# Second MLP of an attention and two-MLP kernel: seven products in one run, then 36 output products in one run

## The chip, the cores and the metric

The kernel runs on one core of one Trainium2 chip. The metric is device time in microseconds (us); before the change the median of three runs is 923.41 (922.23 to 925.97). Nothing is computed on the host.

## What is computed

Kernelized attention for 4 batches of 8 heads, 576 tokens and 64 features; its output, laid out as 2304 tokens of 512 features, goes through two MLPs. The second one is what the change touches:

```python
def _moe_ref(x, w1, w2, w3, w_out):
    a = x @ w1                         # 512 -> 1024
    b = x @ w2
    h = a * b @ w3
    return h @ w_out                   # 1024 -> 512

def _moe2_ref(x, w_in, w_out):
    h = x @ w_in                       # 512 -> 2048
    r = np.maximum(h, 0.0)
    g = r * r
    return g @ w_out                   # 2048 -> 512
```

The second MLP's weights arrive as 64-bit words and are decoded to float32 on the chip.

## The kernel before

**Three stages.** Attention (to about 210 us in the trace), the first MLP (to about 528) and the second MLP (to the end). Each float32 operand is split in a high and a low half, and each product of two tiles is three matmuls (high by high, low by high, high by low; `passes`). Each matmul is preceded by its own weight load, which overlaps the matmul before.

**First MLP.** 40 steps of 36 matmuls (of 512 columns where the batch has 512 tokens): 12 for `pa`, 12 for `pb`, and 12 that fold the gated product g of the step before into four accumulators `yp` (line 984, `fold_part`; here called the fold products). VectorE makes g from `pb` and the copy of `pa`, ScalarE its high half, VectorE its low half (line 1145). In the last two runs of steps the accumulators are added to a partial sum read back from HBM (`yp<-y_part`, line 972). The result goes to HBM as `y_hbm`, in three slabs of 768 tokens.

**Decoding beside it.** The weights of the second MLP are decoded in 32 items, 28, 29, 23 and 26 among the last; the table `many` (line 929) says how many items begin in each step. An item costs VectorE five operations of 128x512 and one or more for its low half, and the results are stored in HBM (`pair_hbm<-w_w`, `<-v_w`, line 809).

**Second MLP.** A slab has 16 blocks of 128 hidden features, taken in eight pairs p; over the three slabs there are 24 pairs q. For a pair the hidden layer is computed with seven products instead of eight (a Strassen-Winograd scheme): the seven *forms* of the slab's activations (b11, t2, b21, t3, t1, b22, t4: sums and differences of quarters, split in halves, tiles yf_b and yf_t) are multiplied by forms of the weights (a11, s2, a12, s3, s1, s4, a22). Each product is six matmuls of 384 columns (line 1221) into one of three banks x (`ph_x`), y (`ph_y`) and w (`ph_w`), where x and y are each added to later: x takes a11 and a12, y takes s2, s3 and a22, w takes s1 and s4. Between them the other engines form the sums: ScalarE copies x to m after a11; VectorE makes u = y + m after s2, m5 = w + m + y, and later w + u and y + m. Each of the four results is squared after a maximum with zero on VectorE (line 1236), its high half r is made on ScalarE (line 1232) and its low half on VectorE (line 1233). Then the 36 output products of 512 columns of that pair (line 1247, `op<-pair,r`: r times the weights `wo`) accumulate into six banks op_0 to op_5 over the eight pairs of a slab; they are issued during the next pair.

**What sets the order.** No scheduler: within the manual sections the instructions stand on each engine in the order in which the program issues them, and a wait holds everything behind it on that engine. `filling` is a list of output products of the pair before; `fill(4)`, `fill(3)`, `fill(2)` and `fill(1)` issue a quarter, a third of the rest, and so on, between the products. The weights of the pairs are loaded by `pump` (line 1056) on SP, in the order of `coming_pairs`, when room for two tiles is free; the first calls stand in `first_forms` (line 933), which also says after which step of the first MLP (30 to 39) each form of the first slab is made. `pair` of tiles 0 and 1 are the seven products' weights (two tiles each, 0_0, 0_1, 1_0, 1_1), 2 and 3 are `wo`.

At the end of a slab (its pairs 6 and 7, and the first pair of the next) the next slab's sums and forms are made between the products (`adding`, `remake`). The last six output tiles are copied out of their banks on ScalarE and VectorE in turn and stored by halves of 64 rows, on SP's and on ScalarE's queue (`put_out`).

## Time and profile before

| | us |
|---|---|
| median of three runs | 923.41 |
| profiled execution | 924.3 |
| its span, first to last instruction | 922.5 |
| TensorE busy | 900.5 |
| VectorE busy | 670.8 |
| ScalarE busy | 379.0 |
| mean granted TensorE clock | 0.995 of 2.4 GHz |

Busy time of TensorE counts a matmul until its modelled end, which overlaps the next one: a busy TensorE need not be at its peak, and the distance between the starts of groups tells more. The chain of waits follows the work back from the last instruction, at each step to what released it. In the timeline a row holds a run of like instructions: its start, its length, and in brackets the idle time before it with what ended that. PEld is the weight load, SPq and ACTq are the issues of transfers on SP and ScalarE.

### The profile page before, as it was taken

Reading aid. Unit: us, or ns where it says so; the run is one execution under the profiler, and the core shown is the slowest. Engines: PE = TensorE matmul, PEld = TensorE weight load, DVE = VectorE, ACT = ScalarE, POOL = GpSimd, SP = SyncE. Lnnn points to the kernel's source line nnn. Section 1 sums busy time; section 2 is a strip of 40 time slices with the busy share of each in tenths; the row PEclk is TensorE's granted clock in tenths of the full one; section 3 lists DMA queues with packets and bytes.
Section 4 is the critical chain, followed back from the end, with each engine's and each line's share of the span. In section 5 each row is a group of like instructions: output and inputs, shape, how many; then the busy total and the mean of one; then the engine's idle time right before and its main releaser. Section 6 shows DMA issues by size and latency. Waiting matters only on the chain.

```text
span 922.5 us, 15634 instructions
## 1 busy us (share of the span) xinstructions
PE 900.5 (98%) x6012; PEld 764.1 (83%) x6012; DVE 670.8 (73%) x1214; ACT 379.0 (41%) x709; POOL 159.5 (17%) x240
## 2 busy tenths in 40 slices
PE   8999999999999999999999989999999999999997
PEld 6777777778888888988888778989898998889896
DVE  6988888879978797789999656476754447554443
ACT  4777777653433434444455322222421213312121
POOL 2666666453222530000000000000000000000000
PEclk9999999999999999999999989999999999999999
DMA  6455465456452346848895967777675675676442
GB/s 190 123 151 157 139 162 153 120 149 160 105 170 83 122 117 213 287 158 248 293 353 205 356 233 269 240 276 249 224 251 206 209 269 179 215 264 226 168 160 68
DMA packets 120089, 182.60 MB, mean 198 GB/s; under 512 B 60304, under 2 KB 79312, under 8 KB 120016
## 3 DMA queue, kind: packets, MB, share of 16 engines
q1 hardware_dynamic: 118912, 180.66, 60.6%
q8 instruction: 47, 0.77, 0.3%
q10 hardware_dynamic: 1104, 0.95, 0.3%
q14 instruction: 26, 0.21, 0.1%
HBM read 140.54 MB, written 40.89 MB: 197 GB/s over the span
## 4 chain that ended last, share of the span: by engine, by line
PE 82%; DVE 8%; DMA 4%; ACT 4%; issue 1%; SPq 0%; ACTq 0%; DVEq 0%
PE op L1247 20%; PE pb L221 10%; PE yp L984 9%; PE pa L221 9%; PE ph_y L1221 7%; PE ph_x L1221 5%; PE ph_w L1221 5%; PE pf L910 5%; PE po L495 2%; PE pk L282 2%; PE pkv L468 2%; PE pq L407 2%; PE pd L515 1%; ACT qp L457 1%; DMA mrow<-mh 1%
## 5 line engine op out<-in xcount | busy, mean ns | idle before, releaser
L1247 PE MATMUL op<-pair,r 128*128 128x512 f32 x864 | 214.8, 393 | 0.0
L1247 PEld LDWEIGHTS op<-pair,r 128*128 128x128 f32 x864 | 161.9, 188 | 29.5
L984 PE MATMUL yp<-g,w3o 128*128 128x512 f32 (+1 forms) x480 | 105.6, 368 | 0.0
L984 PEld LDWEIGHTS yp<-g,w3o 128*128 128x128 f32 x480 | 84.1, 189 | 14.9 <-DVE w3o L187 0.2
L1232 ACT ACTIVATE r<-m 128x384 fp32r<-128x384 f32 x48 | 25.2, 525 | 168.7 <-DVE m L1236 168.7
L221 PE MATMUL pa<-c,w_w12a 128*128 128x512 f32 (+1 forms) x432 | 94.1, 366 | 0.2 <-ACT c L186 0.2
L221 PE MATMUL pb<-c,w_w12b 128*128 128x512 f32 (+1 forms) x432 | 93.6, 366 | 0.0
L1221 PE MATMUL ph_y<-yf_t,pair 128*128 128x384 f32 x432 | 89.2, 341 | 1.8 <-DVE u L1291 1.8
L221 PEld LDWEIGHTS pa<-c,w_w12a 128*128 128x128 f32 x432 | 75.1, 189 | 14.0 <-ACT c L186 0.6
L221 PEld LDWEIGHTS pb<-c,w_w12b 128*128 128x128 f32 x432 | 75.2, 189 | 13.1
L1221 PEld LDWEIGHTS ph_y<-yf_t,pair 128*128 128x128 f32 x432 | 77.8, 191 | 4.8 <-DVE u L1291 2.1
L1221 PE MATMUL ph_x<-yf_b,pair 128*128 128x384 f32 x288 | 59.3, 340 | 3.5 <-ACT m L1287 1.8
L1221 PEld LDWEIGHTS ph_x<-yf_b,pair 128*128 128x128 f32 x288 | 51.7, 191 | 6.9 <-ACT m L1287 2.8
L1143 ACT ACTIVATE g<-g 128x512 fp32r<-128x512 f32 (+1 forms) x39 | 23.0, 589 | 81.8 <-DVE g L1141 81.8
L540 POOL TENSOR_SCALAR rc<-dc 32x9 f32<-32x9 f32 x128 | 44.9, 350 | 55.7 <-DVE dc L530 48.6
L399 ACT ACTIVATE kp<-kp 128x512 f32<-128x512 f32 (+1 forms) x80 | 46.9, 588 | 16.4 <-DVE kp L392 14.4
L1233 DVE TENSOR_TENSOR r<-m,r 128x384 fp32r<-128x384 f32 x48 | 26.8, 559 | 28.4 <-ACT r L1232 28.4
L910 PE MATMUL pf<-w_wo,w3T 128*128 128x512 f32 x192 | 45.0, 390 | 0.0
L1316 DVE TENSOR_TENSOR m<-ph_w,m 128x384 f32<-128x384 f32 x24 | 13.3, 556 | 40.0 <-PE ph_w L1221 40.0
L910 PEld LDWEIGHTS pf<-w_wo,w3T 128*128 128x128 f32 x192 | 36.0, 188 | 7.5
L123 DVE SCALAR_TENSOR_TENSOR dt_w<-raw_w,dt_w 128x512 int32<-128x512 int32 x48 | 39.1, 814 | 1.6
L1141 DVE TENSOR_TENSOR g<-pb,a 128x512 f32<-128x512 f32 (+1 forms) x39 | 24.7, 634 | 19.8 <-PE pb L221 19.5
(169 smaller groups left out, 1528.0 us busy)
## 6 DMA issues: line engine op xcount, KB each, us to landing
pair<-pair_hbm SPq DMA_DIRECT2D x144, 512.0 KB, 6.4
pair_hbm<-w_w SPq DMA_DIRECT2D x32, 512.0 KB, 7.6
raw_w<-in_moe_w_in_dram SPq DMA_DIRECT2D x16, 512.0 KB, 4.0
raw_w<-in_moe_w_out_dram SPq DMA_DIRECT2D x16, 512.0 KB, 5.4
pair_hbm<-v_w SPq DMA_DIRECT2D x16, 512.0 KB
raw_w<-in_moe_w_dram SPq DMA_DIRECT2D x56, 128.0 KB, 3.2
x<-x_hbm SPq DMA_DIRECT2D x12, 512.0 KB
yi<-y_hbm SPq DMA_DIRECT2D x12, 384.0 KB, 8.0
```

The source lines that it names most:

```text
L123: nc.vector.scalar_tensor_tensor(out=t, in0=hi, scalar=-(1 << 31), in1=t, op0=ALU.bitwise_and, op1=ALU.bitwise_or)
L221: nc.tensor.matmul(ps[:, 0:n], a, c, start=kk + i == 0, stop=kk == KD - 1 and i == 2)
L399: nc.scalar.activation(z["kp", j][:, :, s, :], z["kp", j][:, :, 1, :], AF.Exp, scale=1.0 - 2.0 * s)
L540: nc.gpsimd.tensor_scalar(out=z["rc2"][i * 32:(i + 1) * 32, s, :], in0=z["dc"][at * 32:(at + 1) * 32, :], scalar1=1e-6, scalar2=None, op0= ...
L910: nc.tensor.matmul(pf, a, c, start=n == 0, stop=n == len(todo) - 1)
L984: nc.tensor.matmul(blk.yp[i][:, 0:blk.n], a, d, start=c == blk.c0 and s == 0, stop=c == blk.c1 - 1 and s == 2)
L1141: nc.vector.tensor_tensor(out=g32[:, 0:n], in0=pb[:, 0:n], in1=a_sb[:, 0:n], op=ALU.mult)
L1143: nc.scalar.activation(g[:, 0, 0:n], g32[:, 0:n], AF.Copy)
L1221: nc.tensor.matmul(ps_, a, c, start=start and n == 0, stop=n == 5, skip_group_check=not start)
L1232: nc.scalar.activation(r[:, 0], h, AF.Copy)
L1233: nc.vector.tensor_tensor(out=r[:, 1], in0=h, in1=r[:, 0].bitcast(F32), op=ALU.subtract)
L1247: nc.tensor.matmul(z.ops[i], a, d, start=z.p + j + s == 0, stop=z.p == NP2 - 1 and j == 1 and s == 2)
```

## The change

The work is the same, product for product. What is changed is its order, in five places.

1. *Most pairs.* In the first pair, the last, and the pairs 1 to 6 of each slab (`whole`) the seven products come in one run (with a22 ahead of s4), then the output products of the pair before in one run, op_4 and op_5 first. All four squarings (t's among them, now a maximum with zero once more and a product in one operation) stand behind the seventh product on VectorE, then the next slab's sums where due, then the decoding of weights (`work`). Pairs 0 and 7 of a slab keep the old order, but for pair 0 of the first slab and pair 7 of the last.
2. *Put-off squarings.* After pair 0 two, and after pair 7 of a slab one of the four results are left in tiles of their own (`put_off`) and squared during the next pair, behind its u (`done_later`).
3. *The hand-over from the first MLP.* The last fold products come behind all seven products of pair 0; the adds of `yp` to the partial sum are spread between the sums of pair 1 (`carried`).
4. *First forms and loads.* `first_forms` and `many` change, and with them the order of decoded items, of the first slab's forms and of the loads on SP.
5. *The end.* The last output tile is copied by columns, half on VectorE and half on ScalarE, and stored from both queues; the two tiles before it go out on SP alone.

```diff
     many = [
-        2, 2, 2, 2, 2, 2, 2, 2, 2, 1, 2, 2, 1, 1, 1, 1, 0, 1, 2, 0, 0, 0, 1, 0, 2, 2, 1, 2,
+        2, 2, 2, 2, 2, 2, 2, 2, 2, 1, 2, 2, 1, 1, 1, 1, 0, 0, 2, 0, 1, 0, 1, 0, 2, 2, 1, 2,
...
     first_forms = {
-        30: ["load"],
+        31: ["load"],
         32: ["sums", "b22"],
...
-        38: ["b21", "give", "pump0"],
-        39: ["pump1"],
+        37: ["t1", "pump0"],
+        38: ["t4", "pump1"],
+        39: ["b21", "give"],
...
+        if last and i == 2:
+            half = C * D
+            nc.vector.tensor_copy(o[:, 0:half], op[:, 0:half])
+            nc.scalar.copy(o[:, half:], op[:, half:])
+            nc.sync.dma_start(dst[0][:, 0:half], o[:, 0:half])
+            nc.scalar.dma_start(dst[0][:, half:], o[:, half:])
+            return
...
-            (queue_of if last else nc.sync).dma_start(dst[0][half] if len(dst) == 1 else dst[h], o[half])
+            (queue_of if last and i > 2 else nc.sync).dma_start(dst[0][half] if len(dst) == 1 else dst[h], o[half])
...
+        def put_off(z, at):
+            later.append((z, at))
+            room_t[1] -= 1
+            name = f"h_{z.nm}_{at[0]}_{at[1]}"
+            z.h[at] = pools[1].tile([P, 512], I32, tag="dt", bufs=4, name=name).bitcast(F32)[:, 0:WIDE]
...
-                filling += [lambda z=before, i=i, j=j: out_part(z, i, j) for i in range(6) for j in range(2)]
+                filling += [lambda z=before, i=i, j=j: out_part(z, i, j) for i in (4, 5, 0, 1, 2, 3) for j in range(2)]
...
             nc.vector.tensor_tensor(out=u2, in0=y, in1=m1, op=ALU.add)
+            if later:
+                done_later()
             product(x, a12, "b21", False)
...
+            whole = q in (0, last) or p not in (0, NP2 - 1)
+            if whole:
+                nc.vector.tensor_tensor(out=m5, in0=y, in1=m1, op=ALU.add)
+            else:
...
+            if q == 1:
+                carried(range(1))
             x = bank_of(pre, "pre", f"ph_w_{z.nm}")[:, 0:WIDE]
             product(x, s1, "t1", True)
...
+            nc.vector.tensor_tensor(out=m5, in0=x, in1=m5, op=ALU.add)
+            if q == 1:
+                carried(range(1, 4))
+            while later:
+                done_later()
+            if whole:
+                product(y, a22, "t4", False)
+                squared(z, (0, 0))
+                if q == 0:
+                    put_off(z, (0, 1))
+                    put_off(z, (1, 0))
+                nc.vector.tensor_tensor(out=z.h[1, 0], in0=y, in1=m1, op=ALU.add)
+                product(x, s4, "b22", False)
+                nc.vector.tensor_tensor(out=z.h[0, 1], in0=x, in1=u2, op=ALU.add)
+                squared(z, (1, 1))
+                for at in ((0, 1), (1, 0)) if q else ():
+                    squared(z, at)
+                give(*[t_ for x_ in range(2) for t_ in fed[x_]])
+                fill(1)
+                if adding:
+                    wide_sums(raws)
+                work()
```

TensorE in a full pair, here pair 3, from its fourth product on; a row is a run of like matmuls, with tile numbers at the names' ends. Before:

```order
L1221 MATMUL ph_y_3_6723<-yf_t_0_6117,pair_0_1_6568 128x384 x3
L1221 MATMUL ph_y_3_6723<-yf_t_1_6120,pair_1_1_6572 128x384 x3
L1247 MATMUL op_0_6445<-pair_2_0_6575,r_2_0_0_6579 128x512 x3
L1247 MATMUL op_0_6445<-pair_3_0_6577,r_2_1_0_6582 128x512 x3
L1247 MATMUL op_1_6446<-pair_2_0_6575,r_2_0_0_6579 128x512 x3
L1247 MATMUL op_1_6446<-pair_3_0_6577,r_2_1_0_6582 128x512 x3
L1221 MATMUL ph_w_3_6765<-yf_t_0_6029,pair_0_1_6568 128x384 x3
L1221 MATMUL ph_w_3_6765<-yf_t_1_6032,pair_1_1_6572 128x384 x3
L1247 MATMUL op_2_6447<-pair_2_0_6575,r_2_0_0_6579 128x512 x3
```

TensorE at the same place now:

```order
L1234 MATMUL ph_y_3_6726<-yf_t_0_6023,pair_0_1_6574 128x384 x3
L1234 MATMUL ph_y_3_6726<-yf_t_1_6026,pair_1_1_6578 128x384 x3
L1234 MATMUL ph_w_3_6751<-yf_t_0_6192,pair_0_1_6574 128x384 x3
L1234 MATMUL ph_w_3_6751<-yf_t_1_6195,pair_1_1_6578 128x384 x3
L1234 MATMUL ph_y_3_6726<-yf_t_0_6269,pair_0_0_6573 128x384 x3
L1234 MATMUL ph_y_3_6726<-yf_t_1_6272,pair_1_0_6577 128x384 x3
L1234 MATMUL ph_w_3_6751<-yf_b_0_5798,pair_0_1_6574 128x384 x3
L1234 MATMUL ph_w_3_6751<-yf_b_1_5801,pair_1_1_6578 128x384 x3
L1270 MATMUL op_4_6451<-pair_2_0_6581,r_2_0_1_6587 128x512 x3
```

The three groups of output products that stood between the products have moved behind the seventh, and op_4 leads them.

SP's queue where the weights of the first pairs are loaded (`pair_0_0` to `pair_1_1` with a number under 6330, then pair 1's), from the last loads of partial sums on; `w_w_28` and `v_w_28` are the decoded item 28. Before:

```order
L875 DMA yp_1_6144<-y_part_1_4152 128x1024
L809 DMA pair_hbm_0_3220<-w_w_28_6127 128x1024
L809 DMA pair_hbm_0_3220<-v_w_28_6128 128x1024
L111 DMA raw_w_31_6219<-in_moe_w_out_dram 128x512
L809 DMA pair_hbm_1_3221<-w_w_29_6206 128x1024
L809 DMA pair_hbm_1_3221<-v_w_29_6207 128x1024
L1066 DMA pair_0_0_6322<-pair_hbm_0_3192 128x1024
L1066 DMA pair_0_1_6323<-pair_hbm_0_3192 128x1024
L1066 DMA pair_1_0_6326<-pair_hbm_1_3193 128x1024
L1066 DMA pair_1_1_6327<-pair_hbm_1_3193 128x1024
L1066 DMA pair_0_0_6330<-pair_hbm_0_3196 128x1024
L1066 DMA pair_0_1_6331<-pair_hbm_0_3196 128x1024
```

SP's queue there now:

```order
L875 DMA yp_1_6138<-y_part_1_4152 128x1024
L1065 DMA pair_0_0_6198<-pair_hbm_0_3192 128x1024
L1065 DMA pair_0_1_6199<-pair_hbm_0_3192 128x1024
L809 DMA pair_hbm_0_3220<-w_w_28_6121 128x1024
L809 DMA pair_hbm_0_3220<-v_w_28_6122 128x1024
L111 DMA raw_w_31_6217<-in_moe_w_out_dram 128x512
L1065 DMA pair_1_0_6275<-pair_hbm_1_3193 128x1024
L1065 DMA pair_1_1_6276<-pair_hbm_1_3193 128x1024
L1065 DMA pair_0_0_6279<-pair_hbm_0_3196 128x1024
L1065 DMA pair_0_1_6280<-pair_hbm_0_3196 128x1024
L809 DMA pair_hbm_1_3221<-w_w_29_6204 128x1024
L809 DMA pair_hbm_1_3221<-v_w_29_6205 128x1024
```

Pair 0's first two tiles have moved ahead of item 28's stores, its last two and pair 1's first two ahead of item 29's; pair 1's last two stand further down, behind the stores of items 23 and 26.

VectorE from pair 0 to pair 1 (the number after a name's letter is slab and pair: `u_0_1` is u of pair 1; `r_0_1_0` is a low half of pair 0). Before:

```order
L1334 TENSOR_TENSOR m_0_0_6354<-ph_y_0_6356,m_0_0_6354 128x384
L1236 SCALAR_TENSOR_TENSOR m_0_0_6354<-m_0_0_6354 128x384
L1233 TENSOR_TENSOR r_0_1_0_6346<-m_0_0_6354,r_0_1_0_6346 128x384
L972 TENSOR_TENSOR yp_0_6143<-yp_1_0_37_6182,yp_0_6143 128x512
L972 TENSOR_TENSOR yp_0_6143<-yp_1_1_37_6183,yp_0_6143 128x512
L972 TENSOR_TENSOR yp_1_6144<-yp_1_2_37_6184,yp_1_6144 128x512
L972 TENSOR_TENSOR yp_1_6144<-yp_1_3_37_6185,yp_1_6144 128x512
L1291 TENSOR_TENSOR u_0_1_6471<-ph_y_1_6464,m_0_1_6462 128x384
L1295 TENSOR_TENSOR t_1_6479<-t_1_6479 128x384
```

VectorE there now:

```order
L1246 SCALAR_TENSOR_TENSOR m_0_0_6382<-m_0_0_6382 128x384
L1248 TENSOR_TENSOR r_0_1_1_6347<-m_0_0_6382,r_0_1_1_6347 128x384
L1321 TENSOR_TENSOR u_0_1_6473<-ph_y_1_6466,m_0_1_6464 128x384
L1246 SCALAR_TENSOR_TENSOR h_0_0_1_6401<-h_0_0_1_6401 128x384
L1248 TENSOR_TENSOR r_0_0_1_6348<-h_0_0_1_6401,r_0_0_1_6348 128x384
L1332 TENSOR_TENSOR m_0_1_6492<-ph_y_1_6466,m_0_1_6464 128x384
L1215 TENSOR_TENSOR yp_0_6137<-yp_1_0_37_6176,yp_0_6137 128x512
L1350 TENSOR_TENSOR m_0_1_6492<-ph_w_1_6495,m_0_1_6492 128x384
L1215 TENSOR_TENSOR yp_0_6137<-yp_1_1_37_6177,yp_0_6137 128x512
L1215 TENSOR_TENSOR yp_1_6138<-yp_1_2_37_6178,yp_1_6138 128x512
L1215 TENSOR_TENSOR yp_1_6138<-yp_1_3_37_6179,yp_1_6138 128x512
L1246 SCALAR_TENSOR_TENSOR h_0_1_0_6402<-h_0_1_0_6402 128x384
```

u of pair 1 has moved ahead of the four adds of yp and of two of pair 0's squarings (`h_0_0_1`, `h_0_1_0`), and the adds are spread between pair 1's sums.

## Rows read from the trace of the kernel before

**Rows 1.** Busy time by stretch: us, busy us by engine, granted clock, DMA share, GB/s
```profile
528.40:530.80 2.40, 0.68 (x5) 0.35 (x4) 0.00 (x0) 0.00 (x0) 0.00 (x0) 1.00 1.04 410
530.80:534.00 3.20, 3.20 (x12) 2.97 (x13) 0.54 (x1) 0.48 (x1) 0.00 (x0) 0.66 0.98 375
534.00:538.00 4.00, 4.00 (x20) 3.74 (x19) 1.13 (x3) 1.02 (x2) 0.00 (x0) 0.84 0.98 362
```

**Rows 2.** Chain of waits from 500 on: start us, length us, what
```profile
501.33 2.72 PE yp L984 x12
...
563.43 1.04 PE ph_x L1221 x6
...
630.28 2.76 PE op L1247 x12
...
662.21 2.76 PE op L1247 x12
...
673.72 1.04 PE ph_x L1221 x6
677.88 2.76 PE op L1247 x12
```

**Rows 3.** Timeline from the first MLP to the second: start us, length us, instructions
```profile
520.66 0.69 DVE L1145 TENSOR_TENSOR g<-g,g 128x512 fp32r<-128x512 f32 x1 [0.70 <-ACT g L1143]
...
525.65 2.89 PE L984 MATMUL yp<-g,w3o 128*128 128x512 f32 x12
...
530.79 0.47 PEld L1221 LDWEIGHTS ph_x<-yf_b,pair 128*128 128x128 f32 x3 [2.05 <-DMA pair<-pair_hbm]
...
546.07 1.31 PE L1221 MATMUL ph_x<-yf_b,pair 128*128 128x384 f32 x6 [1.45 <-ACT m L1287]
546.16 2.48 DVE L972 TENSOR_TENSOR yp<-yp,yp 128x512 f32<-128x512 f32 x4
...
549.16 2.29 PE L1221 MATMUL ph_y<-yf_t,pair 128*128 128x384 f32 x6 [1.77 <-DVE u L1291]
```

**Rows 4.** Timeline of SP, stores of item 28 and first pair loads
```profile
512.90 0.50 SPq L809 DMA_DIRECT2D pair_hbm<-w_w  x1
...
519.20 12.84 SPq L1066 DMA_DIRECT2D pair<-pair_hbm  x10
```

**Rows 5.** The pair loads' line, 515 to 560
```profile
DMA to landing us min/median/max: 9.2/9.7/10.1
```

**Rows 6.** Timeline of two pairs in the steady part, VectorE and TensorE
```profile
604.34 0.56 DVE L1236 SCALAR_TENSOR_TENSOR m<-m 128x384 f32<-128x384 f32 x1
605.49 0.56 DVE L1233 TENSOR_TENSOR r<-m,r 128x384 fp32r<-128x384 f32 x1 [0.59 <-ACT r L1232]
...
612.37 1.20 PE L1221 MATMUL ph_x<-yf_b,pair 128*128 128x384 f32 x6
612.62 0.56 DVE L1291 TENSOR_TENSOR u<-ph_y,m 128x384 f32<-128x384 f32 x1 [1.23 <-PE ph_y L1221]
```

**Rows 7.** Busy time by stretch, one pair with a decoded weight
```profile
614.61:630.28 15.67, 15.67 (x79) 14.11 (x79) 10.52 (x20) 4.16 (x8) 0.00 (x0) 1.00 0.74 263
```

**Rows 8.** Timeline of TensorE in the first pair of the second slab
```profile
659.86 1.31 PE L1221 MATMUL ph_x<-yf_b,pair 128*128 128x384 f32 x6 [0.17 <-ACT m L1287]
```

**Rows 9.** Timeline of the end, and the line of the last stores
```profile
907.84 9.72 PE L1247 MATMUL op<-pair,r 128*128 128x512 f32 x42
...
918.36 0.59 ACT L1084 COPY o<-op 128x512 f32<-128x512 f32 x1 [1.53 <-DVE o L1086]
918.98 0.50 ACTq L1093 DMA_DIRECT2D out_dram<-o  x1
...
L1093 SPq DMA_DIRECT2D out_dram<-o x10: 466/472/589, 672.6 to 919.0; - x10
```

**Rows 10.** Timeline of SP and VectorE, the first slab's activations (yi)
```profile
453.01 3.94 SPq L1022 DMA_DIRECT2D yi<-y_hbm  x4
...
472.13 1.02 DVE L1037 TENSOR_TENSOR t<-yi 128x384 f32<-128x384 f32 x2
```

More of the change, by code (lines that the diff above doesn't have):

```diff
@@ L1078, in put_out @@
         last = s == len(y_hbm) - 1
-        if last:
+        if last and i > 2:
+            o = late.tile([P, 512], I32, tag="dt", bufs=4, name=f"o_{s}_{i}").bitcast(F32)
+        elif last:
             o = stage.tile([P, 1024], I32, tag="raw", bufs=4, name=f"o_{s}_{i}").bitcast(F32)[:, 0:512]
@@ L1082, in put_out @@
             o = stage.tile([P, 512], I32, tag="dt", bufs=3, name=f"o_{s}_{i}").bitcast(F32)
+        dst = rows_of(s * 2 * WIDE // P + i)
+        if last and i == 2:
[5 more added lines that the diff above has]
+            return
         if i % 2 == 0:
@@ L1086, in put_out @@
             nc.vector.tensor_copy(o, op)
-        dst = rows_of(s * 2 * WIDE // P + i)
         if len(dst) == 1 and not last:
@@ L1202, in attention_then_mlps, with carried @@
         filling = [lambda i=i: fold_part(*carry, i) for i in range(KD)]
-        def carried():
-            give(w3o[carry[1]])
-            finish_block(carry[0])
-        filling.append(carried)
+        def carried(some):
+            blk = carry[0]
+            for i in some:
+                y = blk.part[i // 2]
+                nc.vector.tensor_tensor(out=y[:, i % 2, :], in0=blk.yp[i][:, 0:blk.n], in1=y[:, i % 2, :], op=ALU.add)
+                if i % 2:
+                    store_y(blk.b, blk.n, i // 2, y)
+                    give(y)
+            if 3 in some:
+                give(w3o[carry[1]])
         def fill(share):
@@ L1259, in attention_then_mlps, with work @@
         raws, before = None, None
+        def work():
+            at_work[0].words()
+            at_work[0].tail()
+            at_work[0] = at_work[0].rest(many[len(steps) + q + 1] if q < 15 else 0)
+        at_work, later = [beat], []
         for q in range(last + 1):
@@ L1309, in attention_then_mlps @@
-            beat.words()
-            beat.tail()
-            beat = beat.rest(many[len(steps) + q + 1] if q < 15 else 0)
+            m5 = lunit(F32, [512], f"m5_{z.nm}", "t", 2)[:, 0:WIDE]
+            z.h = {(0, 0): t, (1, 1): m5, (1, 0): m1, (0, 1): u2}
+            whole = q in (0, last) or p not in (0, NP2 - 1)
[3 more added lines that the diff above has]
+                squared(z, (0, 0))
+                if q and p == 0:
+                    form("b22", raws)
+                    form("t4", raws)
+                    give(*raws.tiles)
+                if remake:
+                    form("b11", raws)
+                    wide_last(raws)
+                    form("t2", raws)
+                fill(4)
+                work()
+                nc.vector.tensor_tensor(out=m5, in0=y, in1=m1, op=ALU.add)
@@ L1336, in attention_then_mlps @@
-            give(*[t for x_ in range(2) for t in fed[x_]])
-            fill(1)
+            nc.vector.tensor_tensor(out=m5, in0=x, in1=m5, op=ALU.add)
[5 more added lines that the diff above has]
+                product(y, a22, "t4", False)
+                squared(z, (0, 0))
+                if q == 0:
[11 more added lines that the diff above has]
+                    wide_sums(raws)
+                work()
+            else:
+                squared(z, (1, 1))
+                if remake:
+                    form("b21", raws)
+                    form("t3", raws)
+                fill(3)
+                product(x, s4, "b22", False)
+                nc.vector.tensor_tensor(out=z.h[0, 1], in0=x, in1=u2, op=ALU.add)
+                squared(z, (0, 1))
+                if remake:
+                    form("t1", raws)
+                fill(2)
+                product(y, a22, "t4", False)
+                put_off(z, (1, 0))
+                nc.vector.tensor_tensor(out=z.h[1, 0], in0=y, in1=m1, op=ALU.add)
+                give(*[t_ for x_ in range(2) for t_ in fed[x_]])
+                fill(1)
```

54 lines of the change are left out of this document (11 added, 43 removed).

## The prediction

> **What bounds the kernel now.** I read the busy time by stretches first, then the chain of waits, then the timeline at each place where the chain leaves TensorE. Over the span TensorE is the engine that sets the time; the stretch that concerns us begins when the last twelve fold products of the first MLP's step 39 start at 525.65 [rows 3] and lasts to the end. Inside it there are two different things to see.
>
> In the steady part the chain is TensorE alone. From 662.21 to 677.88, one pair, is 15.67 us [rows 2], with no wait in it. Twelve 512-wide products take 2.72 us in the first MLP (0.2267 each) where only 512-wide ones follow each other, and 2.76 when they stand alone between 384-wide ones; four groups of six 384-wide products in a row, 24 of them, take 677.88 - 673.72 = 4.16 (0.1733 each) [rows 2]. So 36 output products and 42 products should cost 36 x 0.2267 + 42 x 0.1733 = 8.16 + 7.28 = 15.44; the pair takes 0.23 more. It changes width eight times: 0.029 us a change.
>
> At the start of the second MLP the chain is not TensorE. Its first products begin at 528.37 (525.65 + 2.72), stop for pair weights until 530.79, later for ScalarE's copy m until 546.07 (1.45 idle) and for VectorE's sum u until 549.16 (1.77 idle), the latter behind four adds of yp that start at 546.16 [rows 3]. After the wait for weights the granted clock is 0.66 and then 0.84 of 2.4 GHz on average, a mixture of both levels, where it was 1.00 before [rows 1]. Pair 2 begins at 563.43 [rows 2].
>
> **The change, part by part.**
>
> *Start of the second MLP.* From 528.37 to the first product of pair 2 the work is the same in both kernels: 84 products, 12 fold products and 36 output products, 84 x 0.1733 + 12 x 0.2267 + 36 x 0.2267 = 14.56 + 2.72 + 8.16 = 25.44, and four changes of width in the new order, 0.12: 25.6. It took 563.43 - 528.37 = 35.06. So 9.5 us is there to be won, if every wait goes and the clock stays up. What is late next, wait by wait:
>
> Weights. The queue moves pair 0's first two tiles ahead of the stores of item 28, and the last two ahead of the stores of item 29. SP issues item 28's stores from 512.90, so the first two tiles can go near 513; before, the ten pair loads began at 519.20 [rows 4]. Under a full queue (DMA share 1.04 [rows 1]) a load lands 9.2 to 10.1 us after its issue [rows 5]. Two 512 KB transfers fewer stand ahead of the third tile. At the 390 to 410 GB/s of that stretch [rows 1] one is about 1.3 us, so the tile that landed at 530.79 lands near 528.2 and the fourth near 529.5. The products want them at 528.7 and 529.8: just in time. For pair 1 the same count (stores of items 29, 23 and 26 now stand ahead of its last two tiles) gives 538.4 and 539.7 against a need at 538.7 and 539.8. Here I take 0.5 us of waiting together; the ends are 0 and 3.6 (rival 1).
>
> m and u. Pair 0 no longer squares its last two sums before pair 1 begins, so on ScalarE m of pair 1 stands right behind the second r of pair 0, and on VectorE u of pair 1 ahead of the yp adds. With products from 528.4, pair 0's seven end at 535.7, the twelve fold products at 538.4. VectorE is done with the second squaring at about 539 (a squaring is 1.15 from its first operation to its last and 0.48 on to the next [rows 6]) and u is due at 540.6: no wait. The first yp add comes between pair 1's two sums; it is about 0.65 long and makes the last product some 0.3 late. The put-off squarings end near 548.3, the product that reads them stands at 549.2. So 9.5 - 0.5 - 0.3 = **8.7 us** won, between 5.5 and 9.5.
>
> *Seven products in a row.* 18 full pairs lie behind that (2 to 6, 9 to 14, 17 to 23); 7, 8, 15 and 16 keep the old order. Six changes of width fewer each: 6 x 0.029 = 0.17, times 18 = **3.1 us**, between 0 (the excess has another cause) and 4.1 (all 0.23 goes). What hid the sums before was output products; now each sum has one product of cover. The fourth product already lives with that: the third starts at 612.37, u starts at 612.62 and takes 0.56, to 613.18, and the fourth, due at 613.41, was not late [rows 6]. The sixth and the seventh stand in the same relation to their sums. The fifth product takes the bank of x over once ScalarE's t has read it, and has one product of cover too. All four squarings now follow the last product: they end about 13.6 us after the pair's first product, and with the 3.2 us of a decoded weight (10.52 busy in such a pair [rows 7], less 13 operations of 0.56) at 16.9; the next u is due at 15.5 + 2.25 = 17.7. Cover 0.8 us; nothing added, and each 1 us of lateness would cost 1 us in up to six pairs.
>
> *Between slabs.* From 630.28 to 662.21 are two pairs and 0.59 us more [rows 2]: m waits on ScalarE behind pair 7's last r, and the third product of pair 8 starts late at 659.86 [rows 8]. Now that squaring is put off behind u of the next pair. Two such places: **1.1 us**, from 0 to 1.2. The forms of the next slab keep their places there.
>
> *The end.* TensorE ends at 917.56 (907.84 + 9.72). ScalarE copies the last tile only at 918.36, since it first issues a half of the tile before; its store goes at 918.98 [rows 9]. Now these halves go to SP. The two half copies come one behind the other, since ScalarE's waits for VectorE's: about 0.4 + 0.4 from 917.65, to 918.5. But SP now issues five stores in a row from 916.85 at 0.47 each [rows 9], the last at 918.75. SP's is the later: **0.3 us**, between -0.3 (a 1 KB row lands slower) and 0.5.
>
> *In the first MLP.* Decoded items and forms move by a step. The yi loads move from 453.01 by a step of 36 x 0.2267 = 8.2 us, so their four issues end at 465.1; with 9.7 us under way [rows 5] the last lands at 474.8, where VectorE wants it at 473.1 [rows 10]: at worst 1.7 us late. TensorE doesn't see it: VectorE's low half of g is done at 521.35 (520.66 + 0.69) and is used at 525.65 [rows 3], over 4 us of cover. I add nothing; without that cover it would be these 1.7.
>
> Sum: 8.7 + 3.1 + 1.1 + 0.3 = 13.2 us. The profiled execution took 924.3 (span 922.5), 0.9 over the median of 923.41, within the spread of the three runs. 924.3 - 13.2 = 911.1; from the median, **910.3**.
>
> **The rivals.**
> 1. *The weights are late again.* For: the count leaves 0.1 to 0.5 us, and the DMA engines are full either way [rows 1]. Against: the shift by two transfers is sure from the order. If the wait of before stays in one of the two places, 1.9 us (528.9 to 530.8) comes back, and the clock with it: 3.2 us at 0.66 and 4 us at 0.84 lose 1.1 + 0.6. Together 3.6, less the 0.5 already counted: about 913.5; in both, 917.
> 2. *Changes of width cost nothing.* The 0.23 us could belong to the output products as such (their weights, their banks), whatever stands beside them. Then the second term falls out: 910.3 + 3.1 = 913.4. For: 0.029 us is small and I have no row of a change alone. Against: the excess shows in both kinds of group, 2.76 for 2.72 and more than 1.04 for six. The Trainium skill ("TensorE: Matmul & The Clock Gate", section "Back-to-back issue gap") speaks for this rival: it gives a gap by the width of the moving operand plus a constant, with no price for a change.
> 3. *Slower: the seven products wait for the sums.* In 18 pairs the sixth and the seventh product each wait d for VectorE, as the sum has 0.06 us of cover (613.18 to the weight load 0.17 ahead of 613.41). 36 x d equals all that is won at d = 0.37; at d = 0.5 it is 910.3 + 18 = 928. For: the cover is that thin, and VectorE may still be at a decode. Against: the fourth product has the same cover in every pair and no wait shows.
> 4. *The start is not repaired*, since TensorE's waits there move to something I don't see (a bank of the output products, a slot for the weights): the first term is lost, 919.
>
> **How the numbers follow.** Forecast 910.3: 0.66. Rival 1: 0.14; rival 2: 0.10; rival 3: 0.05; rival 4: 0.05. The range: with every term at its best (9.5 + 4.1 + 1.2 + 0.5 = 15.3) the time is 908.1, and runs scatter by 1 to 2 us; upward it takes in rivals 1 (one place) and 2: 907.5 to 915.5. A difference of 0.5%, 4.6 us, is about what can be told from no change: under 918.8 is faster. The forecast, rival 2 and rival 1 lie there, 0.90; rival 4 is within it, 0.05; rival 3 is slower, 0.05.
>
> **What would show it.** Right: in the chain the stretch from the last fold products of step 39 to pair 2's first product falls from 35 to about 26.5 us, with no entry for m or u and the granted clock near 1.00 throughout; a steady pair takes 15.5; the two pairs across a slab's end have no extra 0.6. Wrong: an entry for pair weights of over 1 us and a clock under 0.9 behind it (rival 1); a steady pair still at 15.67 (rival 2); entries of VectorE's sums m or u in each pair (rival 3).

## The result: 913.2 us, and where the time went

The changed kernel takes 913.19 us (median of four executions, 912.77 to 914.46) against 922.82 us for the kernel before on the same chip (921.51 to 925.97): a ratio of 0.9893, 95% interval 0.9866 to 0.9920. The prediction was 910.3 with a range from 907.5 to 915.5: the direction and the range held, the forecast was 2.9 us too low. The two profiled executions took 924.3 and 912.77 us, their spans are 922.5 and 910.7. The 11.8 us between the spans divide like this:

| term of the sum | forecast, us | between the two traces, us |
|---|---|---|
| first MLP, to the last fold products | 0 | 0.4 |
| start of the second MLP | 8.7 | 8.0 |
| seven products in a row, 18 pairs | 3.1 | 2.9 |
| between slabs, two places | 1.1 | 0.7 |
| the end | 0.3 | -0.2 |
| sum | 13.2 | 11.8 |

In the chain of waits of the changed kernel (start us, length us, what) the stretch between the two MLPs and the steady part read:

```profile
525.40 2.72 PE yp L983 x12
528.12 1.02 PE ph_x L1234 x6
...
529.53 0.72 SPq L1065
530.25 0.05 issue
530.30 10.42 DMA pair<-pair_hbm
540.72 0.04 issue
540.77 0.80 PE ph_y L1234 x3
...
546.82 8.20 PE op L1270 x36
555.02 1.06 PE ph_x L1234 x6
...
562.32 8.20 PE op L1270 x36
570.52 1.06 PE ph_x L1234 x6
...
649.41 1.21 PE ph_y L1234 x6
```

From the first product at 528.12 to pair 2's at 555.02 it is 26.90 us, where [rows 2] and [rows 3] gave 563.43 - 528.37 = 35.06. That last figure takes its two ends from two views, the chain and the timeline; with both ends from the timeline it is 563.26 - 528.37 = 34.89 before and 554.86 - 527.96 = 26.90 now, 8.0 us less. The copy m and the sum u, which ended waits of 1.45 and 1.77 us in [rows 3], are no longer in the chain. What is left there is one entry for pair weights. TensorE's own rows in the timeline show how little it waits for them, at two tiles of pair 1:

```profile
539.18 0.79 PE L1234 MATMUL ph_x<-yf_b,pair 128*128 128x384 f32 x3 [0.42 <-DMA pair<-pair_hbm]
...
540.77 0.80 PE L1234 MATMUL ph_y<-yf_t,pair 128*128 128x384 f32 x3 [0.25 <-DMA pair<-pair_hbm]
```

The busy time by stretches (us, busy us by engine, granted clock, DMA share, GB/s) answers to [rows 1]. Where the clock read 1.00, 0.66 and 0.84 it now reads 1.00 throughout, with the DMA engines just as full:

```profile
528.00:530.40 2.40, 2.40 (x15) 2.31 (x14) 1.16 (x4) 0.70 (x2) 0.00 (x0) 1.00 0.92 277
530.40:533.60 3.20, 3.20 (x21) 3.20 (x20) 1.25 (x3) 0.49 (x1) 0.00 (x0) 1.00 1.02 419
533.60:537.60 4.00, 4.00 (x21) 3.60 (x20) 2.82 (x7) 1.05 (x2) 0.00 (x0) 1.00 1.03 421
```

In the kernel before, the clock fell a second time, behind the wait of 1.77 us for u, which neither [rows 1] nor the prediction has:

```profile
548.90:552.30 3.40, 3.14 (x9) 2.95 (x10) 2.73 (x6) 1.09 (x2) 0.00 (x0) 0.50 1.07 320
```

So 3.4 us at half the clock, some 1.7 us lost, stood behind that wait as well as behind the one for weights; both are gone.

A steady pair is 570.52 - 555.02 = 15.50 us, where [rows 2] gave 15.67; its 36 output products in one run take 8.20 against 36 x 0.2267 = 8.16. Across a slab's end two pairs take 31.57 us (first product to first product; 31.93 before), and the trace of what is still lost is the ph_y entry of 1.21 at 649.41, a product that usually takes 1.04.

The timeline of SP shows the queue at the start, with the time to landing on the pair loads' line (answering to [rows 4] and [rows 5]):

```profile
525.63 3.85 SPq L809 DMA_DIRECT2D pair_hbm<-w_w  x2
529.53 11.57 SPq L1065 DMA_DIRECT2D pair<-pair_hbm  x10
```

```profile
DMA to landing us min/median/max: 10.4/10.7/11.0
```

Pair 0's four tiles and pair 1's first two were issued ahead of these rows (two from 512.23, four from 520.00). The next ten loads begin at 529.53, behind the last stores of decoded items; the first of them is the tile that pair 1 wants at 538.8, the second the other late one.

The end, in the timeline (it answers to [rows 9]):

```profile
905.52 0.42 DVE L1087 COPY o<-op 128x256 f32<-128x256 f32 x1
905.98 0.37 ACT L1088 COPY o<-op 128x256 f32<-128x256 f32 x1 [1.23 <-DVE o L1087]
906.38 0.36 ACTq L1090 DMA_DIRECT2D out_dram<-o  x1
907.26 0.54 SPq L1089 DMA_DIRECT2D out_dram<-o  x1
```

TensorE ends at 905.49. ScalarE's half is issued 0.9 us later, VectorE's, though copied first, 1.8 us later: SP is still issuing the stores of the tiles before. The span ends at 910.7, 5.2 behind TensorE, where it was 4.96.

### The profile page after: what moved, and what is told of

The parts are those of the page before. It is cut to its first block, busy times and chain, and to the rows that moved or that the text cites. A ratio compares the mean times of both kernels' runs of the same rounds, so it can differ in the third digit from the quotient of the medians.

```text
span 910.7 us, 15658 instructions
## 1 busy us (share of the span) xinstructions
PE 893.7 (98%) x6012; PEld 760.7 (84%) x6012; DVE 660.0 (72%) x1215; ACT 378.2 (42%) x709; POOL 159.2 (17%) x240
## 4 chain that ended last, share of the span: by engine, by line
PE 87%; DVE 5%; DMA 3%; ACT 3%; issue 1%; SPq 0%; DVEq 0%
PE op L1270 22%; PE pb L221 10%; PE yp L983 10%; PE pa L221 10%; PE ph_y L1234 8%; PE ph_x L1234 5%; PE ph_w L1234 5%; PE pf L910 5%; PE po L495 2%; PE pk L282 2%; PE pkv L468 2%; PE pq L407 2%; ACT qp L457 2%; PE pd L515 2%; DMA pair<-pair_hbm 1%; ACT kp L399 1%
## 5 line engine op out<-in xcount | busy, mean ns | idle before, releaser
L1270 PE MATMUL op<-pair,r 128*128 128x512 f32 x864 | 202.9, 390 | 0.0
L1234 PE MATMUL ph_y<-yf_t,pair 128*128 128x384 f32 x432 | 87.2, 336 | 0.3 <-DMA pair<-pair_hbm 0.3
L1321 DVE TENSOR_TENSOR u<-ph_y,m 128x384 f32<-128x384 f32 x24 | 13.4, 558 | 71.4 <-PE ph_y L1234 70.1
L1247 ACT ACTIVATE r<-m 128x384 fp32r<-128x384 f32 x43 | 22.6, 525 | 73.6 <-DVE m L1246 73.6
L1317 ACT COPY m<-ph_x 128x384 f32<-128x384 f32 x24 | 11.5, 481 | 78.0 <-PE ph_x L1234 78.0
L1248 DVE TENSOR_TENSOR r<-m,r 128x384 fp32r<-128x384 f32 x43 | 24.0, 559 | 25.4 <-ACT r L1247 25.4
```

What stands on the lines that cost most here:

```text
L1234: nc.tensor.matmul(ps_, a, c, start=start and n == 0, stop=n == 5, skip_group_check=not start)
L1247: nc.scalar.activation(r[:, 0], h, AF.Copy)
L1248: nc.vector.tensor_tensor(out=r[:, 1], in0=h, in1=r[:, 0].bitcast(F32), op=ALU.subtract)
L1270: nc.tensor.matmul(z.ops[i], a, d, start=z.p + j + s == 0, stop=z.p == NP2 - 1 and j == 1 and s == 2)
```

## The experiments on the start

The theory was that the late weights, the waits for sums and the low clock behind them each held a share of the 9.5 us. Two runs take the change apart: the new places of forms and loads alone, put into the kernel before, and the new order of the second MLP alone, with the old places.

**loads_alone.** The kernel before, with the tables `many` and `first_forms` of the changed kernel:

```
...
     first_forms = {
-        30: ["load"],
+        31: ["load"],
...
-        38: ["b21", "give", "pump0"],
-        39: ["pump1"],
+        37: ["t1", "pump0"],
+        38: ["t4", "pump1"],
+        39: ["b21", "give"],
```

> The kernel before, with one part of the change alone: the places of the first forms, of the pair loads and of the decoded items in the first MLP's last steps (the tables many and first_forms). The first products of the second MLP took 35.06 us to pair 2 in the kernel before and 26.90 in the changed one. Theory, weights and sums each have a share: the wait for pair weights at 528.9 (1.9 us) and the low clock behind it (1.7 us) go, the waits for m (1.45) and u (1.77) stay: 31.2 to 31.8 from the first product to pair 2, and 3 to 4 us under the kernel before. Rival A, the loads alone do it and the waits for m and u were a consequence of the late start: 27 to 28. Rival B, the loads do nothing, since the last tile is as late as before: 34.5 to 35.5.

Measured: 930.02 us, 1.0056 of the kernel before (1.0039 to 1.0073). None of the three expectations holds; from pair 0's first product to pair 2's it takes 42.5 us, and this part of the change makes the old order **slower** by 6 us. The first row is TensorE's, from the timeline; the second lists what SP's DMA queue waited for (line, releaser: us in total, times, longest); the third is a stretch with its clock:

```profile
553.09 1.33 PE L1220 MATMUL ph_x<-yf_b,pair 128*128 128x384 f32 x3 [11.67 <-DMA pair<-pair_hbm]
```

```profile
SPq L953 <- DVE yp L971: 23.3, 4, 15.8
```

```profile
553.09:556.34 3.25, 3.25 (x10) 3.25 (x11) 0.00 (x0) 0.48 (x1) 0.00 (x0) 0.50 1.02 417
```

Pair 1 stands 11.67 us before its third tile, and the next 3.25 us run at 0.50, the lower of the clock's two levels. Who is to blame is in the middle row: L953 stores the results y of the last fold products. The two stores wait up to 15.8 us on SP for VectorE's adds of yp, and in the old order pair 1's last tiles are queued behind them on SP. In the kernel before, all of pair 1's loads were issued before those stores; the new places moved them behind. The Trainium skill says the same of the mechanism in "DMA: Bandwidth & Descriptors", section "Anatomy of one DMA — SWDGE (gpsimd) path": DMA engines don't wait on semaphores, the wait is the issuing sequencer's, before it dispatches; the trace agrees for SP's queue, with these 15.8 us. Pair 0's fourth tile is late in this run too, by 1.38 us at 531.85, though its load has the place that it has in the changed kernel, where it was in time.

**order_alone.** The opposite: the changed kernel with the two old tables.

> The changed kernel with the old places of first forms, pair loads and decoded items (the tables many and first_forms of the kernel before). Theory: the products of pair 0 wait again for their third and fourth tile, 1.9 us, the clock falls behind it, 1.7 us more, and m and u stay unwaited for: 26.9 + 3.6 = 30.5 from the first product to pair 2, 3.6 us over the changed kernel. Rival A, the loads are worth everything: 34.5 to 35.5 and 8 us over. Rival B, the order is worth everything, and the tiles wait costs only itself: 28.8, with the clock at 1.00.

Measured: 916.98 us, 0.9919 (0.9904 to 0.9934), about 4 us over the changed kernel. From the timeline, two waits of TensorE, and the clock behind the first:

```profile
530.36 0.79 PE L1235 MATMUL ph_x<-yf_b,pair 128*128 128x384 f32 x3 [1.75 <-DMA pair<-pair_hbm]
...
562.23 1.32 PE L1235 MATMUL ph_y<-yf_t,pair 128*128 128x384 f32 x6 [1.61 <-DVE u L1322]
```

```profile
530.36:532.70 2.34, 2.34 (x10) 2.10 (x11) 0.00 (x0) 0.48 (x1) 0.00 (x0) 0.82 0.98 361
532.70:536.00 3.30, 3.30 (x14) 3.30 (x13) 0.56 (x1) 0.49 (x1) 0.00 (x0) 0.61 0.97 314
```

The wait of 1.75 us comes back, and the clock falls behind it, as the theory says. The start, from 527.82 to 557.31, takes 29.49, not 30.5, because the old places also spare pair 1 its two waits (it takes 15.54 us to pair 2's first product, against 16.78 in the changed kernel); behind the start u of pair 2 is late by 1.61 instead, behind a decoded item that the old table puts into pair 1. So the order gives about two thirds of the change by itself, and the loads the rest, but only behind the new order.

What in the new order carries it? Pair 0's last squarings are put off, and VectorE's adds of yp stand behind u of pair 1, with their stores. Two runs put these back.

**adds_behind_folds.**

```
...
+        filling.append(lambda: carried(range(4)))
...
-            if q == 1:
-                carried(range(1))
...
-            if q == 1:
-                carried(range(1, 4))
```

> The changed kernel, but VectorE's four adds of the last fold products again stand in one piece right behind them, ahead of u of pair 1; pair 0's last two squarings stay put off. Theory: the adds, 0.65 each, begin as the first fold bank ends and are done at about 540.9, u of pair 1, due at 540.6, ends near 541.4: the fourth product of pair 1 waits 0.5 us, at most 1.8, and the start takes 27.4 to 28.7 instead of 26.90. Rival, the adds have slack in this place and only the put-off squarings made room: 26.9 plus or minus 0.2.

Measured: 924.62 us, some 11 over the changed kernel, and 37.42 us for the start: both expectations fail. The chain:

```profile
539.30 2.48 DVE yp L1215 x4
...
541.80 0.37 SPq L953
...
542.77 6.57 DMA pair<-pair_hbm
549.34 0.04 issue
549.39 1.33 PE ph_x L1236 x3
```

VectorE's adds, the two y stores that wait for them on SP, pair 1's tiles behind the stores, then TensorE: the same stall as in loads_alone.

**adds_and_squares_behind.** As before, and pair 0's last two sums are squared at once (no `put_off` at q = 0).

> As the run with the adds behind the fold products, and pair 0's last two sums are squared at once too, ahead of the adds (two squarings of some 1.6 us on VectorE, with ScalarE's copy of each in front of m of pair 1). Theory: m of pair 1 waits again (1.45 us in the kernel before), and u is 2 to 3.3 us late: the start takes 29.0 to 31.5, and the clock falls under 1.00 behind the wait. Rival, what was put off has slack here as long as the weights are in time: under 27.5.

Measured: 927.55 us; pair 1 waits 12.95 us for its weights. The squarings ahead of the adds push the y stores back by 3 us more, and the start with them.

**adds_behind_stores_later.** The deciding one: the adds stay right behind the fold products, their stores and the release of their tiles go back behind pair 1's loads.

```
...
+        def added():
+            blk = carry[0]
+            for i in range(KD):
+                y = blk.part[i // 2]
+                nc.vector.tensor_tensor(out=y[:, i % 2, :], in0=blk.yp[i][:, 0:blk.n], in1=y[:, i % 2, :], op=ALU.add)
+
+        filling.append(added)
...
-                nc.vector.tensor_tensor(out=y[:, i % 2, :], in0=blk.yp[i][:, 0:blk.n], in1=y[:, i % 2, :], op=ALU.add)
...
-            if q == 1:
-                carried(range(1))
...
             if q == 1:
-                carried(range(1, 4))
+                carried(range(4))
```

> VectorE's four adds of the last fold products in one piece right behind them, as in the run adds_behind_folds, which took 11 us more than the changed kernel; but the two stores of their results on SyncE stay behind pair 1's loads, where the changed kernel has them. Theory formed on that run: the stall of 9.4 us is SyncE's, whose two stores wait for the adds with the loads of pair 1's last tiles queued behind them; with the stores behind the loads the tiles are loaded from about 529.5 as in the changed kernel, the stall falls to 0.4 to 0.9 us, the start takes 26.9 to 28.0, and what is left over 26.90 is the price of the adds on VectorE alone (0 to 1.1). Rival, the tiles' slots or VectorE itself hold pair 1 up: a wait of several us for pair weights or for u stays.

Measured: 912.41 us (span 910.3), and one wait at the start:

```profile
538.89 0.79 PE L1241 MATMUL ph_x<-yf_b,pair 128*128 128x384 f32 x3 [0.83 <-DMA pair<-pair_hbm]
```

The start takes 554.23 - 527.31 = 26.92 against 26.90. The place of the adds on VectorE costs nothing that can be read; the place of their **stores** on SP, ahead of or behind pair 1's loads, is worth 10.5 us of the start (37.42 against 26.92). How much the putting-off of pair 0's squarings is worth by itself, no run shows: the run without it has the stores in front as well.

## The experiments on the steady part and the slab ends

**split_again.** 17 pairs go back to eight changes of width:

```
...
-            whole = q in (0, last) or p not in (0, NP2 - 1)
+            whole = q in (0, 1, last)
...
-                put_off(z, (1, 0))
+                if p in (0, NP2 - 1):
+                    put_off(z, (1, 0))
...
+                if p not in (0, NP2 - 1):
+                    squared(z, (1, 0))
+                if adding:
+                    wide_sums(raws)
```

> The changed kernel, but pairs 2 to 6 of the first slab and 1 to 6 of the others (17 pairs) again take their last three products between output products (8 changes of moving width a pair instead of 2); start, slab ends and tail stay as changed. Theory, a change of moving width costs 0.029 us: 15.67 from pair to pair instead of 15.51, and the whole 17 x 0.16 = 2.7 us longer than the changed kernel. Rival, changes of width are free and the gain lay elsewhere: 15.5 a pair and the same time as the changed kernel.

Measured: 919.72 us (eight executions), 0.9949 (0.9934 to 0.9965), so 6.5 over the changed kernel and not 2.7. The chain over an undisturbed pair:

```profile
555.93 1.06 PE ph_x L1234 x6
...
560.12 2.76 PE op L1270 x12
...
563.95 2.08 PE op L1270 x9
...
570.24 1.39 PE op L1270 x6
571.63 1.04 PE ph_x L1234 x6
...
587.30 1.04 PE ph_x L1234 x6
```

587.30 - 571.63 = 15.67: the 0.16 us a pair come back as the theory says, 2.7 in all. The rest is no price of width. My edit leaves the next slab's sums in one piece at the end of a slab's seventh pair, where no run of output products now covers them, and the next u is late (1.15 us of idle time in the row below, 2.4 us in all at the two places); pair 5 loses 0.3 to a decoded weight. The start (27.33 us) and the first MLP were 0.9 us longer here without an edit there: in the seven traces that have the changed kernel's start it took from 26.65 to 27.33, as pair 1's tiles were more or less late.

```profile
638.92 1.32 PE L1234 MATMUL ph_y<-yf_t,pair 128*128 128x384 f32 x6 [1.15 <-DVE u L1321]
```

**finely_mixed.** Three output products behind every three product matmuls (the order in which the output products come changes with it):

```
...
                     n += 1
+                if between and filling:
+                    filling.pop(0)()
...
```

> The changed kernel, but in the same 17 pairs three output products stand behind every three product matmuls from the second product's first half on: 24 changes of moving width a pair instead of 2, the same 78 matmuls. Theory, each change costs 0.029 us whatever lies around it: 22 x 0.029 = 0.64 more, 16.15 a pair, 17 x 0.64 = 10.9 us longer than the changed kernel. Rival A, the cost belongs to the seam behind a finished product (its last matmul and the wait behind it), not to the width: about as many finished products as before, so 15.5 to 15.7 a pair. Rival B, changes of width are free: 15.5.

Measured: 960.18 us, 1.0392 (1.0370 to 1.0414). Most of this is no price of width. With the output run gone from behind the seven products, the next pair's third product waits for ScalarE's copy m, which stands behind the squarings of the pair before (1.65 us here):

```profile
576.61 0.79 PE L1234 MATMUL ph_x<-yf_b,pair 128*128 128x384 f32 x3 [1.65 <-ACT m L1327]
```

I had not expected this stall, and it is not that of rival 3 (the sixth and the seventh product waiting for their sums): the squarings stand behind the seventh product, and it is the run of 36 output products behind it that gives them their time. The first such pair has no wait in it, and shows the width alone, in the stretch table and the chain:

```profile
555.56:571.30 15.74, 15.74 (x79) 14.13 (x78) 4.52 (x10) 2.02 (x4) 0.00 (x0) 1.00 0.49 166
```

```profile
556.79 0.52 PE ph_y L1234 x3
557.31 0.70 PE op L1272 x3
558.01 0.53 PE ph_y L1234 x3
558.54 0.69 PE op L1272 x3
```

It takes 15.74 with 24 changes of width. Two changes gave 15.50, eight 15.67, so a constant 0.029 each would have given 16.15. The 22 further changes cost 0.011 each, and rival B (15.5) is wrong as well; rival A, the seam behind a finished product, misses its upper end by 0.04 only, but its mark, runs behind a finished product that cost more than others, isn't there (0.70 and 0.69 after unfinished and finished ones). What the runs of output products have above 0.2267 each: 0.015 for 3 (0.695), 0.03 for 6 (1.39), 0.04 for 9 and for 12 (2.08, 2.76), 0.04 for 36 (8.20). So the price of a change isn't paid at the change. It builds up over the nine products behind it and then ends; a run of three pays only the beginning. The starts of the single products in the changed kernel's trace say the same: in the run of 36 the first nine follow each other by 0.224 to 0.236 us, from the tenth on by 0.226 or 0.227. Nor is it the change to other weights and banks, since that costs nothing where the width stays, as in the changed kernel's first MLP (chain):

```profile
506.37 2.72 PE pb L221 x12
509.09 2.72 PE yp L983 x12
```

Why the width matters for nine products is not settled by these runs.

**slab_squared_at_once.** No putting off at slab ends:

```
...
-                put_off(z, (1, 0))
                 nc.vector.tensor_tensor(out=z.h[1, 0], in0=y, in1=m1, op=ALU.add)
+                squared(z, (1, 0))
```

> The changed kernel, but at the ends of slabs (pairs 7, 8, 15 and 16) the last sum is squared at once again instead of behind u of the next pair. In the changed kernel the stretch from pair 7's first product to pair 9's is 31.57 us, in the kernel before 31.93. Theory, the put-off squaring frees ScalarE for m: 31.9 again at both places, 0.7 us over the changed kernel in all. Rival, the gain there came from the order of output and pair products and the squaring has slack: 31.5 to 31.6.

Measured: 912.75 us. Pair 7's first product to pair 9's is 663.84 - 631.79 = 32.05, 0.48 over the changed kernel's 31.57 and even over the 31.93 before; at the next slab's end it is 32.05 too. The wait is back, in the place of [rows 8] and with the same length:

```profile
650.12 1.32 PE L1234 MATMUL ph_x<-yf_b,pair 128*128 128x384 f32 x6 [0.17 <-ACT m L1317]
```

The total doesn't show it (912.75 in one execution), since the start was 0.25 us shorter here and the first MLP ended 0.4 sooner, which is what executions of one kernel differ by.

## The experiments on the end, and a better version

**tail_before.** The changed kernel with the old way of writing the last tiles.

```
...
-        if last and i == 2:
-            half = C * D
-            nc.vector.tensor_copy(o[:, 0:half], op[:, 0:half])
-            nc.scalar.copy(o[:, half:], op[:, half:])
...
-            (queue_of if last and i > 2 else nc.sync).dma_start(dst[0][half] if len(dst) == 1 else dst[h], o[half])
+            (queue_of if last else nc.sync).dma_start(dst[0][half] if len(dst) == 1 else dst[h], o[half])
```

> The changed kernel with the last outputs written as before (whole-tile copies, each tile's two halves sent by SyncE and by ScalarE's queue). In the changed kernel the time from the last product's end (905.49) to the span's end (910.70) is 5.21 us, in the kernel before 4.94. Theory, the last product's output waits in SyncE's issues: with the older writing SyncE ends its issues sooner and the stretch is 4.9 to 5.0, the span 0.2 to 0.3 shorter. Rival, the 0.27 is how long a landing happens to take from run to run: the stretch stays at 5.1 to 5.3.

Measured: 913.11 us; TensorE ends at 906.07, the span at 911.02: 4.95 us, as in the kernel before. This part of the change is a loss of some 0.2 us, and not what a landing happens to take: over all runs, nine traces with the changed kernel's end have 5.14 to 5.22 us there, the three with the old one 4.95 or 4.96.

**tail_whole.** Two stores fewer on SP:

```
-        if len(dst) == 1 and not last:
+        if len(dst) == 1 and (not last or i < 2):
```

> The changed kernel, but the last output tiles 0 and 1 go out in one transfer each instead of two half-partition ones, all on SyncE, so that SyncE issues two transfers of some 0.55 us fewer ahead of the half of the last tile. Theory, issues on SyncE set the end: the last issue starts at the last product's end plus 0.6 instead of plus 1.77, and the end is then set by ScalarE's half (issued 0.89 behind the last product); the stretch from the last product to the end is 4.1 to 4.3 instead of 5.21, the span about 1.0 shorter. Rival, landings set the end (the queues share the transfer of the earlier tiles): within 0.2 of 5.2.

Measured: 911.64 us. In the timeline SP's three last issues and ScalarE's:

```profile
905.15 1.13 SPq L1097 DMA_DIRECT2D out_dram<-o  x2
...
906.37 0.41 SPq L1089 DMA_DIRECT2D out_dram<-o  x1
906.76 0.36 ACTq L1090 DMA_DIRECT2D out_dram<-o  x1
```

The first of these rows is two issues with a pause between them; the line of the whole tiles gives what one takes (min/median/max in ns):

```profile
L1097 SPq DMA_DIRECT2D out_dram<-o x12: 332/338/385, 660.1 to 905.9; - x12
```

TensorE ends at 905.86, SP's last issue starts 0.5 us behind it, and the span ends at 909.9: 4.0 us instead of 5.2. A whole tile of 128 x 512 is issued in 0.34 us, where a half of 64 x 512 takes 0.55 (the line of the changed kernel below). The idea of the halves was sound; the two queues' share of the issues was not.

**changed_again** and **changed_improved.** The second has the whole tiles of the last run and two edits more:

```
-        39: ["b21", "give"],
+        39: ["b21", "give", "pump1"],
...
-                if remake:
-                    form("t1", raws)
                 fill(2)
                 product(y, a22, "t4", False)
                 put_off(z, (1, 0))
                 nc.vector.tensor_tensor(out=z.h[1, 0], in0=y, in1=m1, op=ALU.add)
+                if remake:
+                    form("t1", raws)
```

> The changed kernel once more, on the same chip as the version that follows: 0.987 to 0.992 of the kernel before, start 26.9 us, 0.4 to 0.9 of it waiting for pair 1's last two tiles, 5.2 us behind the last product.

> The changed kernel with three edits. Pair 1's last two tiles are loaded ahead of the stores of items 23 and 26: theory, the two waits of 0.42 and 0.25 us go, 0.5 to 0.9 us. Output tiles 0 and 1 of the last slab go out whole: 1.0 to 1.2 us, as in the run tail_whole. At slab ends VectorE takes the sum h ahead of the low halves of form t1, so that its bank is free in time: 0.2 us at each of two places. In all 1.7 to 2.5 us under the changed kernel. Rival for the loads: the stores of items 23 and 26, now two transfers later, are read back by pairs soon after and come late there; a wait for weights of over 1 us in pair 2 or 3 and no gain.

Measured side by side: the changed kernel 912.76 us, 0.9881 (0.9866 to 0.9895); the improved one 910.40 us, 0.9859 (0.9842 to 0.9875). The four executions of one (911.65 to 913.07) and of the other (910.28 to 910.87) don't overlap: 2.4 us, within what was expected. By the traces the end gives 1.2 (4.0 behind TensorE's last product), the slab ends 0.2 each (31.4), and the start 0.3 (26.51 against 26.80), 1.9 in all; the rest is the first MLP, which ended sooner in these executions without an edit there. Of these only the end and the slab ends are clear; 0.3 is less than the start differs by from trace to trace. At the start the wait mostly moved: pair 1 waits for nothing and takes 15.53 us instead of 16.73, but pair 0's fourth tile is late,

```profile
529.91 0.79 PE L1234 MATMUL ph_y<-yf_t,pair 128*128 128x384 f32 x3 [0.48 <-DMA pair<-pair_hbm]
```

and pair 0 takes 10.98 us instead of 10.07.

## Why the prediction was right, and where it was off

*What bounds the kernel.* Right: every place in which the change won time was one where the chain left TensorE or where TensorE changed width.

*The start, 8.7 against 8.0.* The size was nearly right. Pair 0's tiles were in time, as counted from the queue, but with some luck: with the same places for its loads the fourth was 1.38 us late in loads_alone and 0.48 in changed_improved. Pair 1's two late tiles cost more than I took. The 0.67 us of idle time is 1.2 us from start to start, since each wait also brings a slower restart (0.79 for three products that take 0.68 else), and that is nearly all of the 1.3 us over the ideal 25.6. I took 0.5 for it, and 0.3 for a first yp add that made no product late. A misreading played little part: the rates in [rows 1] are 410, 375 and 362 GB/s, not 390 to 410, which moves my count for the tiles by 0.3 us at most. The step that failed is the account of **why** it is won. I put the moved adds down to VectorE (u ahead of the yp adds) and gave pair 1's tiles only the stores of items 29, 23 and 26 ahead of them. The y stores are issued by the same moved step, and I did not count them on SP: with the adds in front they stand ahead of pair 1's tiles and cost 10.5 us, while the adds themselves cost nothing that can be read (adds_behind_stores_later). That the whole new order removes the waits for m and u is shown (neither stands in the start of order_alone); which part of it does so, the put-off squarings or another, is not. In the sum the omission did no harm, since the change moves the stores behind. But I treated loads and sums as separate gains; loads_alone shows that the new loads without the new order lose 6 us. Rival 1 named the right resource, the weights, and the wrong threat to them.

*Seven products in a row, 3.1 against 2.9.* Right, and rival 2 fell: split_again gives 15.67 back, against the Trainium skill, "TensorE: Matmul & The Clock Gate", section "Back-to-back issue gap", whose formula makes the gap of an isolated matmul its width's time and a constant; the trace (15.67 and 15.50 for the same 78 matmuls) decides. But the price per change was right only for runs like the kernel's, of six products and more; finely_mixed shows 0.011 for runs of three. Rival 3 did not come: the sixth and the seventh product take 1.04 as the others do. What finely_mixed ran into is another stall, of squarings without the run of output products behind them.

*Between slabs, 1.1 against 0.7.* The cause was right (slab_squared_at_once); I didn't see that the sum h of pair 7, whose bank the next pair's ph_y takes, now ends behind the low halves of form t1 on VectorE. That leaves 0.17 us at each place, and moving h ahead of the form wins it (changed_improved).

*The end, 0.3 against -0.2.* Wrong in sign. The step was the row of SP's issues: I took five at 0.47 us. On the same line they now take

```profile
L1101 SPq DMA_DIRECT2D out_dram<-o x11: 466/553/597, 656.1 to 906.6; - x11
```

0.55 (min/median/max in ns), so the last starts 1.8 us behind TensorE's end and not 1.2. The 0.47 was the median of issues that mostly had a pause before them; in the kernel before too, those straight behind another took up to 0.59 [rows 9]. The term measured lies near the lower bound of -0.3, but not for the reason given with it: the last store did not land more slowly (the span ends 3.4 us behind the start of the last issue, 3.5 before).

*From the sum to the time.* The terms were 1.4 us too large. The rest of the 2.9 lies in the two medians: against the trace's own execution the forecast was 911.1 for a measured 912.77, while the median of the kernel before in these sessions was anything from 922.8 to 924.1.

## What to carry to other kernels

When a step moves, follow each DMA that it issues to the queue on which it will wait: a store that waits for an engine holds up every load behind it on that queue, and here that was worth 10.5 us where the adds themselves are 2.5 us of VectorE's time. Changes that reorder loads and changes that reorder their competitors belong together: here the new loads alone cost 6 us, and behind the new order they won 4. And count the issues that remain on a queue at the very end, since a half-tile took more issue time here than a whole one (0.55 and 0.34 us).

## What was not expected of the hardware

A stream of matmuls that changes from 384 to 512 wide runs slow for nine products behind the change, not at it (0.015 us lost in three, 0.04 in nine or more). SP took 0.55 us to issue a store of 64 x 512 here, and only 0.34 for one of 128 x 512. And behind a wait of 1.75 us for weights the granted clock read 0.82 and then 0.61 for some 5.6 us, while behind the changed kernel's waits of 0.42 and 0.25 it stayed at 1.00. The lower level cost some 1.7 us there (2.34 x 0.18 + 3.30 x 0.39), as much again as the wait that it followed. A long wait didn't always bring it: behind order_alone's second wait, 1.61 us for u, the clock stayed at 1.00, and so it did in finely_mixed behind one of 2.49 us that ended at 931.20.
